# Gated mix of dilated attention and a token-mixing MLP on one core: the gate row spread by GpSimd, the biases loaded by quarters and turned by VectorE

## The chip, the core and the metric

The kernel runs on one core of a Trainium2 chip. A core has a matrix engine (TensorE, PE in the profile, with its weight loads listed as PEld), a vector engine (VectorE, DVE), an engine for functions of one input (ScalarE, ACT), a general engine (GpSimd, POOL) and an engine that here only issues transfers (SyncE, SP). Each has its own queue of instructions and runs them in order; they wait for each other through semaphores. PE writes only to PSUM, which has eight banks; the other data lie in SBUF, with 128 partitions. The metric is the device time of one execution in microseconds (us).

## What is computed

With x of 2048 tokens by 512 channels, the output is `g * a + (1 - g) * b`:

```python
g = _sigmoid((x * gate_w).sum(-1, keepdims=True))     # one gate for each token
# a: 32 heads of 16 channels; token s looks at s, s-2, ..., s-14
qkv = x @ wqkv                                        # 512 -> 1536
logits = einsum("bhsd,bhswd->bhsw", q, kg) * scale    # 8 places, masked where s - 2w < 0
a = einsum("bhsw,bhswd->bhsd", softmax(logits), vg) @ wo
# b: an MLP over the tokens, for each channel
h = _layernorm(x)
u = _gelu(einsum("bsd,sf->bdf", h, w1) + b1)          # 2048 -> 1792
b = transpose(einsum("bdf,fs->bds", u, w2) + b2)      # 1792 -> 2048
```

All inputs and the output are bf16. Two vectors matter here: `gate_w`, 512 values that every partition needs as a row, and the biases `b1` (1792) and `b2` (2048), which the kernel needs as columns: 14 columns of 128 for b1 (B1C) and 16 for b2 (B2C), one value for each partition.

## The kernel before

Tokens lie on the partitions in 16 tiles of 128 (X). PE's program has these stages, in this order: an opening (five warming products, the transposes tx0 to tx3 of the first four x tiles, and the "lead" products, which multiply the first four normalised tiles with the first 512 columns of w1 into banks 0 to 3); the projections of q, k and v (L713); the first MLP product, ph2 (L609), with two short sums over q·k products (sum0 and sum1, L803) in between; and the second MLP product, ph3 (L937), to which the attention output times wo (L946) is added in the same bank. ACT evicts the projections and takes the functions; VectorE multiplies q with shifted k (128 x 4096 elements at a time), does the softmax arithmetic and multiplies attention with shifted v; some of the wide sums are done by GpSimd's accumulating transfers (L831, L901).

The opening is a chain over four tiles. For tile t, VectorE takes statistics (st), their aggregate (ag, L627); ACT makes the reciprocal deviation with two functions (rstd: Ln and Exp); VectorE normalises the tile (ln, L634); PE runs lead t. ACT and VectorE also copy the transposed x tiles out of PSUM (ext0 to ext3, L598 on VectorE); the projections need these copies.

The gate row and the biases come in through the opening too. GpSimd fills a 128 x 512 buffer with zeros (GWZ, L478), ACT's queue loads the gate row into its first partition (L533), PE multiplies it with a matrix of ones, so that each partition gets the row (gwbc, L643, into bank 6), and ACT copies it to GWB (evgw, L656). The biases are loaded as 14 and 16 rows of 128 (B1R and B2R, L534 and L535, on ACT's queue), PE transposes both into bank 7 (L602 and L603, between tx1 and tx2), and VectorE copies them out (L674, L675), right after the last normalised tile. Then VectorE runs the gate's sums z0 to z15 (L756), one for each x tile: a product of the tile with GWB, summed along the row. z0 to z3 come first; z4 and z5, and the statistics st4 and st5, need x tiles 4 and 5, which are loaded later. A small reduction (RP, L679) and the q·k products follow.

The order on each queue is not the order of the code. A planner (`_Sched`) collects all operations with an assumed duration, their reads and writes, a priority and at times a delay, plays them through a model, and gives each engine its list: whichever ready operation can start first, and among those the one with the longest remaining path. Operations named in `after` fix an order only; `reads`, `writes` and `deps` become waits. PE's list is held in the order of the code, apart from the two sums. So a changed duration or dependency on one engine can change the places of operations that the diff does not show: here those of the q·k products among the statistics, and of sum0 and sum1 among the ph2 products.

GpSimd's queue holds, in order: the fills, the affine select that makes the identity (L475), the fills for padding and mask, and then transfers only: the accumulate of the first q·k products (qd0, L831, 2 MB), two more of 1 MB, the spreading of the attention weights (L880) and the accumulates over v (L901). SP's queue holds all other loads.

Of the kernel before, what the change touches and what calls it, by code (L numbers as in the profile page):

```python
# [5 lines left out]
BF16 = mybir.dt.bfloat16  # L6
# [3 lines left out]
AF = mybir.ActivationFunctionType  # L10
# [3 lines left out]
D = 512  # L14
# [4 lines left out]
NST = S // 128  # L19
# [271 lines left out]
class _Mem:  # L291
# [17 lines left out]
    def view(self, name, dtype, dims, extra=0, p0=0, np_=128):  # L309
        base = self.arena[:].bitcast(dtype)  # L310
        pst = base.ap[0][0]
        esz = mybir.dt.size(dtype)
        o = self.off[name]
        assert o % esz == 0
        return bass.AP(base.tensor, p0 * pst + o // esz + extra, [[pst, np_]] + [list(d) for d in dims])


def bass_gated_mix__sliding_local_dilated__mixer_token_mlp__prompt_kernel(nc, A_x, A_wqkv, A_wo, B_x, B_w1, B_b1, B_w2, B_b2, gate_w, out, dbg=None):
    with contextlib.ExitStack() as es:
# [37 lines left out]
        def psub(ap_, p0, np_, offs, dims):  # L357
            pst = ap_.ap[0][0]
            return bass.AP(ap_.tensor, ap_.offset + p0 * pst + offs, [[pst, np_]] + [list(d) for d in dims])
# [51 lines left out]
        E32 = view("E32", FP32, [(1, D)])  # L411
        GWB = view("GWB", BF16, [(1, D)])
        LX = view("LX", BF16, [(D, NLEAD), (1, D)])
        GWZ = view("LOG", BF16, [(1, D)], extra=NLEAD * 128 * GL)
        GW1 = psub(GWZ, 0, 1, 0, [(1, D)])
        JUNK = view("S4", BF16, [(D, 4), (1, D)])
        ZN = view("Z", FP32, [(1, 32)])
        TZ = view("Z", FP32, [(1, 32)], extra=32)
# [4 lines left out]
        ONES4 = view("ONES", BF16, [(0, 4), (1, 128)])  # L423
        RP = view("RP", BF16, [(1, 32)])
        MASK = view("MASK", BF16, [(PAD, NW), (1, PAD)], np_=32)
        B1R = view("ROWS", BF16, [(1, 128)], np_=NFT)
        B2R = view("ROWS", BF16, [(1, 128)], extra=128, np_=NST)
        so = [0]

        def small(n, dims=None, extra=0):  # L430
# [30 lines left out]
        def psb(bank):  # L461
            return ps[:, bank, :].bitcast(BF16)

        def sub(ap_, offs, dims):
            return bass.AP(ap_.tensor, ap_.offset + offs, [list(ap_.ap[0])] + [list(d) for d in dims])
# [4 lines left out]
        def act(o_, i_, f_, **kw):  # L470
            return lambda e: e.activation(out=o_, in_=i_, func=f_, **kw)  # L471
# [3 lines left out]
        A("pool", lambda e: e.affine_select(out=IDENT, in_=ONES, pattern=[[1, 128]], compare_op=ALU.is_equal,  # L475
                                            fill=0.0, base=0, channel_multiplier=-1),
          0.4, reads=["ones"], writes=["ident"], name="ident")
        A("pool", lambda e: e.memset(GWZ, 0.0), 0.4, writes=["gwr"], name="gwz", prio=-50)  # L478
        A("pool", lambda e: e.memset(sub(KH[0], 0, [(KR, 4), (1, PAD)]), 0.0), 0.2, writes=["kpad"], name="kpad")  # L479
        A("pool", lambda e: e.memset(sub(V5, 0, [(VR, 4), (1, PAD)]), 0.0), 0.2, writes=["vpad"], name="vpad")  # L480

# [12 lines left out]
        def load(name, dst, src, nbytes, writes, transpose=False, queue="sp", issue=0.5, order=True, deps=(), reads=()):  # L494
            ds = sch.dsem(name)

            def fn(e):
                if transpose:
                    return e.dma_start_transpose(dst, src)
                return e.dma_start(dst, src)  # L500
            op = sch.dma(queue, fn, nbytes, ds, issue=issue, reads=reads, writes=writes, deps=deps,
                         after=([last_ld[0]] if order and last_ld[0] is not None else []), name=name)
            if order:
                last_ld[0] = op
            return op
# [25 lines left out]
        ld_w("wk01", 1, 0, 2, "wk")  # L531
        ld_w("wk23", 1, 2, 4, "wk2")
        load("gw", GW1, bass.AP(gate_w.tensor, gate_w.offset, [[D, 1], [1, D]]), 1024, ["gwr"], issue=0.4, queue="act", order=False)  # L533
        load("b1", B1R, B_b1.rearrange("(t p) -> t p", p=128), 4096, ["b1r"], issue=0.4, queue="act", order=False)  # L534
        load("b2", B2R, B_b2.rearrange("(t p) -> t p", p=128), 4096, ["b2r"], issue=0.4, queue="act", order=False)  # L535
        ld_w("wq01", 0, 0, 2, "wq")
        ld_x(4, 2)
        ld_w("wq23", 0, 2, 4, "wq2")
# [25 lines left out]
        def f_warm(n, bank):  # L564
# [4 lines left out]
                return ins  # L569
            return fn  # L570

        chain = [None]

        def PE(fn, dur, reads, writes, name, prio=0):
            op = A("pe", fn, dur, reads=reads, writes=writes, after=([chain[0]] if chain[0] is not None else []), name=name, prio=prio)
            chain[0] = op
            return op
# [12 lines left out]
        def tx(t):  # L590
            PE(f_tx(t), 0.4, ["x%d" % t, "ident"], ["b%d" % TXB[t][0]], "tx%d" % t)

        def ext(t, eng, after):
            bank, o = TXB[t]
            src = sub(psb(bank), o, [(128, 4), (1, 128)])
            dst = sub(XT, t * 128, [(S, 4), (1, 128)])
            if eng == "dve":
                return A("dve", lambda e: e.tensor_copy(out=dst, in_=src), 0.42, reads=["b%d" % bank], writes=["xt0_%d" % t], after=after, name="ext%d" % t, prio=-30)  # L598
            return A("act", act(dst, src, AF.Copy), 0.6, reads=["b%d" % bank], writes=["xt0_%d" % t], after=after, name="ext%d" % t, prio=-30)

        def f_tb(e):
            e.transpose(out=psb(7)[:, 512:512 + NFT], in_=B1R, identity=IDENT[0:NFT, 0:NFT])  # L602
            return e.transpose(out=psb(7)[:, 544:544 + NST], in_=B2R, identity=IDENT[0:NST, 0:NST])  # L603

        def f_ph2(ft, bank, s0, s1):
            def fn(e):
# [22 lines left out]
        def rstd(t, after=()):  # L629
            A("act", act(col(SD, t), AG[:, t, 1:2], AF.Ln, bias=1e-5), 0.25, reads=["ag%d" % t], writes=["sd%d" % t], after=after, name="lnl%d" % t, prio=-40)  # L630
            return A("act", act(col(RSTD, t), col(SD, t), AF.Exp, scale=-0.5), 0.25, reads=["sd%d" % t], writes=["rstd%d" % t], name="rs%d" % t, prio=-40)

        def apply(t, after):
            return A("dve", (lambda t_: lambda e: e.tensor_scalar(out=LX[:, t_, :], in0=X[:, t_, :], scalar1=AG[:, t_, 0:1], scalar2=col(RSTD, t_),  # L634
                                                                  op0=ALU.subtract, op1=ALU.mult))(t), 0.41, reads=["rstd%d" % t, "st%d" % t, "x%d" % t],
                     writes=["lx%d" % t], after=after, name="ln%d" % t, prio=-40)

        PE(f_warm(5, 0), 2.1, [], ["b0"], "warm0")
        tx(0)
        tx(1)  # L640
        PE(f_tb, 0.2, ["b1r", "b2r", "ident"], ["b7"], "t_b12")
        tx(2)
        PE(lambda e: e.matmul(ps[:, 6, :], lhsT=WONE, rhs=GWZ, start=True, stop=True), 0.4, ["gwr"], ["b6"], "gwbc")  # L643
        def lead(t):
            PE(f_lead(t), 0.87, ["lx%d" % t, "lw%d" % t], ["b%d" % ft for ft in range(GL)], "lead%d" % t)

# [6 lines left out]
        lead(0)  # L653
        ag = aggr(1, [l0])
        r1 = rstd(1)
        ew = A("act", act(GWB, ps[:, 6, :], AF.Copy), 0.6, reads=["b6"], writes=["gwb"], after=[r1], name="evgw", prio=-50)  # L656
        tx(3)
        s2 = stat(2, [ag])
        l1 = apply(1, [s2])
        lead(1)  # L660
        ag = aggr(2, [l1])
        r2 = rstd(2)
        s3 = stat(3, [ag])
        l2 = apply(2, [s3])
        ag = aggr(3, [l2])
        e1 = ext(1, "act", [r2, e0])
        r3 = rstd(3, [e1])
        ext(2, "act", [r3])
        e3 = ext(3, "dve", [ag])
        l3 = apply(3, [e3])  # L670
        e3 = l3
        lead(2)
        lead(3)
        A("dve", lambda e: e.tensor_copy(out=B1C, in_=psb(7)[:, 512:512 + NFT]), 0.15, reads=["b7"], writes=["b1c"], after=[e3], name="b1c", prio=-20)  # L674
        A("dve", lambda e: e.tensor_copy(out=B2C, in_=psb(7)[:, 544:544 + NST]), 0.15, reads=["b7"], writes=["b2c"], after=[e3], name="b2c", prio=-20)  # L675

        def f_rp(e):
            with nc.allow_low_precision(reason="exact 0/1 indicator sums"):
# [400 lines left out]
```

## Time and profile before

| what | us |
|---|---|
| median of three runs (lowest, highest) | 163.34 (163.06, 163.67) |
| the profiled execution | 162.99 |
| its span, first to last instruction | 161.7 |
| PE busy | 158.7, 98% |
| VectorE busy | 150.9, 93% |
| ACT busy | 77.5, 48% |
| GpSimd busy | 27.2, 17% |

The span is what the profile's times refer to; the 1.3 us between it and the profiled execution lie outside the instructions shown. TensorE ran at its full clock throughout (granted 1.000). A line of the profile gives the source line, the engine, the operation with its shapes, and a count; a line in order of time begins with start and duration. An idle time in brackets stands ahead of the instruction that ended it, with what it waited for. Instructions that only wait, issue a semaphore or load code for an engine are not shown as busy. A transfer's time is given from its issue to its landing.

### The profile page before, as it was taken

What the parts mean: (1) busy time and instruction counts of PE and PEld (TensorE: products, weight loads), DVE (VectorE), ACT (ScalarE), POOL (GpSimd) and SP (SyncE); (2) the same over time, 40 slices, a digit from 0 to 9 for tenths busy, and PEclk for the clock granted to TensorE, in tenths of its full rate; (3) what the DMA queues carried; (4) which work ended last, traced back from release to release, by engine and by line L of the source; (5) the groups of instructions that cost most, each with busy time, mean ns of one, the idle gap of its engine ahead of it and who ended that gap; (6) DMA issues with size and microseconds to landing.
All of it is one profiled execution on the core that took longest, in us unless ns stands there. A gap on an engine that the chain in (4) does not pass through costs nothing.

```text
span 161.7 us, 2009 instructions
## 1 busy us (share of the span) xinstructions
PE 158.7 (98%) x778; PEld 75.9 (47%) x778; DVE 150.9 (93%) x143; ACT 77.5 (48%) x103; POOL 27.2 (17%) x63
## 2 busy tenths in 40 slices
PE   7999999999999999999999999999999999999994
PEld 3455555555554444444444444444444444444652
DVE  2969999999999999999999999999999999999943
ACT  3827666679999381999311344420111111111153
POOL 4000011000000001200792030008580003020000
DMA  4899999999924999999399999999999913949504
GB/s 133 260 228 267 190 295 292 252 212 216 321 92 111 308 292 245 163 296 190 78 321 360 336 298 294 214 311 290 344 206 214 199 50 78 186 109 211 134 32 162
DMA packets 45303, 35.54 MB, mean 220 GB/s; under 512 B 8045, under 2 KB 42094, under 8 KB 45294
## 3 DMA queue, kind: packets, MB, share of 16 engines
q1 hardware_dynamic: 41392, 22.75, 53.4%
q0 software_dynamic: 3696, 12.59, 36.3%
q8 instruction: 6, 0.10, 0.2%
q10 hardware_dynamic: 206, 0.08, 0.2%
q14 instruction: 3, 0.02, 0.0%
HBM read 19.15 MB, written 2.11 MB: 131 GB/s over the span
## 4 chain that ended last, share of the span: by engine, by line
PE 98%; DVE 0%; issue 0%
PE ps L937 30%; PE ps L609 28%; PE ps L713 26%; PE ps L946 9%; PE ps L618 2%; PE ps L568 1%; PE ps L803 1%; PE ps L586 1%; DVE arena L955 0%; PE ps L643 0%; PE ps L602 0%; PE ps L603 0%
## 5 line engine op out<-in xcount | busy, mean ns | idle before, releaser
L468 DVE TENSOR_TENSOR arena<-arena 128x4096 bf16<-128x4096 bf16 (+6 forms) x71 | 125.7, 1807 | 1.5 <-DMA arena<-arena 0.3
L937 PE MATMUL ps<-arena 128*128 128x512 bf16 (+2 forms) x238 | 50.2, 366 | 0.0
L471 ACT ACTIVATE arena<-ps,arena 128x512 bf16<-128x512 f32 (+1 forms) x29 | 20.9, 727 | 55.5 <-PE ps L946 40.6
L609 PE MATMUL ps<-arena 128*128 128x512 bf16 x208 | 45.4, 379 | 0.0
L713 PE MATMUL ps<-arena 128*128 128x512 bf16 x192 | 41.6, 379 | 0.0
L471 ACT ACTIVATE arena<-ps 128x512 bf16<-128x512 f32 (+3 forms) x38 | 31.5, 843 | 14.4 <-PE ps L713 11.2
L937 PEld LDWEIGHTS ps<-arena 128*128 128x128 bf16 x238 | 23.3, 98 | 25.4
L609 PEld LDWEIGHTS ps<-arena 128*128 128x128 bf16 x208 | 20.2, 98 | 24.9 <-issue 0.8
L713 PEld LDWEIGHTS ps<-arena 128*128 128x128 bf16 x192 | 21.7, 113 | 19.7
L880 POOL DMA_DIRECT2D arena<-arena x32 | 17.1, 664 | 23.1 <-DVE arena L468 14.0
L471 ACT ACTIVATE arena<-arena 128x512 bf16<-128x512 bf16 (+6 forms) x27 | 15.2, 565 | 10.1 <-DVE arena L468 9.2
L946 PE MATMUL ps<-arena 128*128 128x512 bf16 (+2 forms) x68 | 15.6, 366 | 0.0
L831 POOL DMA_DIRECT2D arena<-arena x3 | 3.8, 1270 | 62.3 <-DVE arena L468 62.3
L1028 ACT ACT_TABLE_LOAD x9 | 11.5, 1283 | 2.3 <-POOL arena L479 2.2
L756 DVE CUSTOM_DVE_ANT_0 arena<-arena 128x512 bf16<-128x512 bf16 x16 | 10.2, 688 | 1.3 <-DMA arena<-in_A_x_dram 1.3
L901 POOL DMA_DIRECT2D arena<-arena x4 | 4.9, 1226 | 31.4 <-DVE arena L468 31.4
L946 PEld LDWEIGHTS ps<-arena 128*128 128x128 bf16 x68 | 6.6, 98 | 7.2
L775 DVE BATCH_NORM_STATS2 arena<-arena 128x6 f32<-128x512 bf16 x12 | 7.3, 677 | 0.0
L623 DVE BATCH_NORM_STATS2 arena<-arena 128x6 f32<-128x512 bf16 x4 | 2.7, 669 | 2.9 <-DMA arena<-in_A_x_dram 2.9
L955 DVE TENSOR_SCALAR arena<-ps,arena 128x512 bf16<-128x512 f32 (+1 forms) x2 | 1.3, 660 | 3.1 <-PE ps L946 3.0
L618 PE MATMUL ps<-arena 128*128 128x512 bf16 x16 | 4.0, 381 | 0.0
L568 PE MATMUL ps<-const-bfloat16-1.0 128*128 128x512 bf16 x5 | 2.3, 624 | 0.8 <-PEq L1064 0.8
(39 smaller groups left out, 19.0 us busy)
## 6 DMA issues: line engine op xcount, KB each, us to landing
arena<-in_B_w_dram SPq DMA_DIRECT2D x8, 896.0 KB, 13.3
arena<-arena POOLq DMA_DIRECT2D x6, 1024.0 KB, 9.2
arena<-in_B_w_dram SPq DMA_DIRECT2D x5, 1024.0 KB, 8.8
arena<-arena POOLq DMA_DIRECT2D x32, 128.0 KB, 7.3
arena<-arena POOLq DMA_DIRECT2D x1, 2048.0 KB, 17.9
out_dram<-arena SPq DMA_DIRECT2D x15, 128.0 KB, 2.6
arena<-in_B_w_dram SPq DMA_DIRECT2D x2, 768.0 KB, 13.6
arena<-in_A_wqkv_dram SPq DMA_DIRECT2D x4, 256.0 KB, 5.2
```

The lines of the kernel that those rows point to most:

```text
L468: return lambda e: e.tensor_tensor(out=o_, in0=a_, in1=b_, op=op_)
L471: return lambda e: e.activation(out=o_, in_=i_, func=f_, **kw)
L609: ins = e.matmul(ps[:, bank, :], lhsT=W1S[W1AT[ft // 2]][:, st, 128 * (ft % 2):128 * (ft % 2) + 128], rhs=(LX if st < NLEAD else X)[:, st, :],
L618: ins = e.matmul(ps[:, ft, :], lhsT=LW[:, t, 128 * ft:128 * ft + 128], rhs=LX[:, t, :], start=(t == 0), stop=False)
L713: ins = e.matmul(ps[:, bank, :], lhsT=sub(WQKV, dt * 3 * D + tn * D + dl, [(4, 128)]), rhs=XT[:, dt, sb * 512:(sb + 1) * 512], start=(dt = ...
L756: A("dve", (lambda t_: lambda e: e.tensor_tensor_reduce(out=JUNK[:, t_ % 4, :], in0=X[:, t_, :], in1=GWB, scale=1.0, scalar=0.0, op0=ALU.m ...
L775: A("dve", (lambda t_: lambda e: e.bn_stats(out=ST6[:, t_, :], in_=X[:, t_, :]))(t), 0.6, reads=["x%d" % t], writes=["st%d" % t], after=[e ...
L880: prev = sch.dma("pool", (lambda d_, s_: lambda e: e.dma_start(d_, s_))(dst, src), 131072, ds, issue=1.0, reads=["att%d" % h], writes=["av ...
L901: sch.dma("pool", (lambda d_, s_: lambda e: e.dma_start(d_, s_, accum_op=ALU.add, max_dma_last_dim=4096))(sub(PB[b], 0, [(2048, 2), (1, 20 ...
L937: ins = e.matmul(ps[:, bank, 0:c1 - c0], lhsT=W2S[i // 2][:, ft, 128 * (i % 2):128 * (i % 2) + 128], rhs=UT[:, ft, c0:c1], start=(ft == 0) ...
L946: ins = e.matmul(ps[:, bank, 0:c1 - c0], lhsT=OT[:, i // 2, dl, 128 * (i % 2):128 * (i % 2) + 128], rhs=WO[:, dl, c0:c1], start=False, sto ...
L1028: e.preload_act_table_set(want)
```

## The change

The gate row no longer goes through PE. It is still loaded into one partition by ACT's queue; there is no zero fill. GpSimd's `partition_broadcast` writes it to all partitions of GWB. That operation is given a dependency on the last normalised tile of the opening (l3).

The biases leave ACT's queue. After the broadcast GpSimd fills a 128 x 64 buffer (BROW) with zeros and issues eight loads on its own queue: for each quarter of 32 partitions, 14 rows of 32 values of b1 and 16 rows of 32 values of b2. VectorE transposes the buffer in blocks of 32 x 32 (BCOL), so that quarter q of the partitions gets the values 32q to 32q + 31 of each row of 128, and copies the columns to B1C and B2C. The transpose has a delay of 2.0 in the planner.

PE's opening loses the two bias transposes and the product with ones, and gets two filler products of 128 and 256 columns, whose results are not used. ext1 moves ahead of rstd 2 on ACT, and ext3 moves from VectorE to ACT.

In the order that the planner then gives, GpSimd's broadcast, fill and eight loads stand ahead of qd0, and an instruction that loads the code for the broadcast stands before it. VectorE runs RP ahead of z0; after z4 and z5 it runs two q·k products (before: four), the statistics st6 to st9, the bias transpose and the copy of B1C, more statistics, z6 and z7, and only then the other two q·k products of the first pair, which qd0 waits for. PE's sum0 and sum1 stand eight ph2 products later.

```diff
-        GWZ = view("LOG", BF16, [(1, D)], extra=NLEAD * 128 * GL)
-        GW1 = psub(GWZ, 0, 1, 0, [(1, D)])
+        GW1 = view("LOG", BF16, [(1, D)], extra=NLEAD * 128 * GL, np_=1)
...
-        B1R = view("ROWS", BF16, [(1, 128)], np_=NFT)
-        B2R = view("ROWS", BF16, [(1, 128)], extra=128, np_=NST)
+        BROW = view("ROWS", BF16, [(1, 64)])
+        BCOL = view("ROWS", BF16, [(1, 64)], extra=64)
...
-        A("pool", lambda e: e.memset(GWZ, 0.0), 0.4, writes=["gwr"], name="gwz", prio=-50)
...
-        load("b1", B1R, B_b1.rearrange("(t p) -> t p", p=128), 4096, ["b1r"], issue=0.4, queue="act", order=False)
-        load("b2", B2R, B_b2.rearrange("(t p) -> t p", p=128), 4096, ["b2r"], issue=0.4, queue="act", order=False)
...
+        def f_fill(n, bank):
+            return lambda e: e.matmul(ps[:, bank, 0:n], lhsT=WONE, rhs=WROW[:, 0:n], start=True, stop=True)
...
-        def f_tb(e):
-            e.transpose(out=psb(7)[:, 512:512 + NFT], in_=B1R, identity=IDENT[0:NFT, 0:NFT])
-            return e.transpose(out=psb(7)[:, 544:544 + NST], in_=B2R, identity=IDENT[0:NST, 0:NST])
...
         tx(0)
+        PE(f_fill(128, 0), 0.1, [], ["b0"], "fill0")
         tx(1)
-        PE(f_tb, 0.2, ["b1r", "b2r", "ident"], ["b7"], "t_b12")
+        PE(f_fill(256, 0), 0.2, [], ["b0"], "fill1")
         tx(2)
-        PE(lambda e: e.matmul(ps[:, 6, :], lhsT=WONE, rhs=GWZ, start=True, stop=True), 0.4, ["gwr"], ["b6"], "gwbc")
...
-        ew = A("act", act(GWB, ps[:, 6, :], AF.Copy), 0.6, reads=["b6"], writes=["gwb"], after=[r1], name="evgw", prio=-50)
...
-        r2 = rstd(2)
+        e1 = ext(1, "act", [r1, e0])
+        r2 = rstd(2, [e1])
...
-        e1 = ext(1, "act", [r2, e0])
-        r3 = rstd(3, [e1])
-        ext(2, "act", [r3])
-        e3 = ext(3, "dve", [ag])
-        l3 = apply(3, [e3])
+        e2 = ext(2, "act", [r2])
+        r3 = rstd(3, [e2])
+        ext(3, "act", [r3])
+        l3 = apply(3, [ag])
+        gwp = A("pool", lambda e: e.partition_broadcast(GWB, GW1), 0.5, reads=["gwr"], writes=["gwb"], deps=[l3], name="gwb")
+        A("pool", lambda e: e.memset(BROW, 0.0), 0.15, writes=["brow"], after=[gwp], name="brow0")
+        for q_ in range(4):
+            for n_, b_, c_, k_ in (("b1", B_b1, 0, NFT), ("b2", B_b2, 32, NST)):
+                load("%s_%d" % (n_, q_), psub(BROW, 32 * q_, k_, c_, [(1, 32)]), bass.AP(b_.tensor, b_.offset + 32 * q_, [[128, k_], [1, 32]]),
+                     64 * k_, ["%sr%d" % (n_, q_)], queue="pool", issue=1.0, order=False, deps=[gwp], reads=["brow"])
...
-        A("dve", lambda e: e.tensor_copy(out=B1C, in_=psb(7)[:, 512:512 + NFT]), 0.15, reads=["b7"], writes=["b1c"], after=[e3], name="b1c", prio=-20)
-        A("dve", lambda e: e.tensor_copy(out=B2C, in_=psb(7)[:, 544:544 + NST]), 0.15, reads=["b7"], writes=["b2c"], after=[e3], name="b2c", prio=-20)
+        A("dve", lambda e: e.transpose(out=BCOL, in_=BROW), 0.15, reads=["brow"] + ["b%d%s%d" % (n_, "r", q_) for n_ in (1, 2) for q_ in range(4)], writes=["bcol"], after=[e3], name="btr", prio=-30, delay=2.0)
+        A("dve", lambda e: e.tensor_copy(out=B1C, in_=sub(BCOL, 0, [(1, NFT)])), 0.07, reads=["bcol"], writes=["b1c"], name="b1c", prio=-30)
+        A("dve", lambda e: e.tensor_copy(out=B2C, in_=sub(BCOL, 32, [(1, NST)])), 0.07, reads=["bcol"], writes=["b2c"], name="b2c", prio=-30)
```

## The prediction

> **What bounds the kernel now.** I read the page's engine shares first, then the chain that ended last in order of time, then VectorE's instructions in order of time, GpSimd's likewise, and last the DMA issues of the opening.
>
> ```profile
> PE 158.7 (98%) x778; PEld 75.9 (47%) x778; DVE 150.9 (93%) x143; ACT 77.5 (48%) x103; POOL 27.2 (17%) x63
> ```
>
> TensorE (PE) is busy for 98% of the span, VectorE (DVE) for 93%. Chain in order of time (start, us, what):
>
> ```profile
> 4.16 0.12 PE ps L602
> 4.28 0.03 PE ps L603
> 4.30 0.46 PE ps L586 x4
> 4.77 0.22 PE ps L643
> 4.98 0.87 PE ps L618 x4
> ...
> 8.88 41.44 PE ps L713 x192
> ...
> 154.39 5.20 PE ps L946 x28
> ```
>
> From 8.88 on PE runs without a gap, so only two things can move the end: the opening before 8.88, or an input that reaches PE late. VectorE and GpSimd in order of time (start, us, engine, line, what; in brackets the idle time ahead of it):
>
> ```profile
> 1.26 0.20 POOL L474 MEMSET arena<- 128x128 bf16 x1
> 1.54 0.29 POOL L475 TENSOR_SCALAR_AFFINE_SELECT arena<-arena 128x128 bf16<-128x128 bf16 x1
> 2.46 0.14 POOL L480 MEMSET arena<- 128x56 bf16 x1
> 4.34 0.41 DVE L634 TENSOR_SCALAR arena<-arena 128x512 bf16<-128x512 bf16 x1
> 7.37 0.41 DVE L634 TENSOR_SCALAR arena<-arena 128x512 bf16<-128x512 bf16 x1 [0.20 <-ACT arena L471]
> 7.86 0.68 DVE L756 CUSTOM_DVE_ANT_0 arena<-arena 128x512 bf16<-128x512 bf16 x1
> 11.66 0.69 DVE L756 CUSTOM_DVE_ANT_0 arena<-arena 128x512 bf16<-128x512 bf16 x1 [1.27 <-DMA arena<-in_A_x_dram]
> 14.07 0.28 DVE L679 TENSOR_REDUCE arena<-arena 128x32 bf16<-128x128 bf16 x1
> 14.29 8.90 DVE L468 TENSOR_TENSOR arena<-arena 128x4096 bf16<-128x4096 bf16 x4
> 23.51 1.42 POOL L831 DMA_DIRECT2D arena<-arena  x1 [20.91 <-DVE arena L468]
> 153.76 1.94 DVE L468 TENSOR_TENSOR arena<-arena 128x2048 bf16<-128x2048 bf16 x2
> ```
>
> VectorE is the second bound. It waits 1.27 us for x tile 4 at 11.66, starts the q·k products at 14.29, and from there to 155.70 waits only 0.29 us. Its last sum (avc6) ends at 153.76 + 1.94 = 155.70. PE needs it for wo12, the fourth of the final tiles: 154.39 + 3 x 0.867 = 156.99. Less a hand-over of 0.06 us (the normalised tile ends at 7.78, PE's load of it starts at 7.84), **VectorE may be 1.23 us late**; beyond that the end moves one for one.
>
> **The change, part by part.** The sum is made against the profiled execution, 162.99 us (span 161.7 and 1.3 around it); the median of the runs is 163.34, 0.35 above.
>
> *PE's opening.* It loses L602, L603 and L643, 0.12 + 0.03 + 0.22 = 0.37 us, and gains two fillers of 128 and 256 columns, at the 0.216 us pace of 512 columns 0.16. But the first lead product starts when the first normalised tile ends (4.34 + 0.41 = 4.75; it starts at 4.81), and the others wait for later tiles. So nothing is gained; the bound is a gain of 0.21.
>
> *ACT and the evictions.* The gate eviction (evgw) goes and ext3 comes from VectorE, 0.58 us each; ext1 takes the free slot at 5.22, and the last ext still ends at 7.82. The last normalised tile waits for ACT's rstd (7.34), not for the ext3 that stood ahead of it. Zero; the cover is lead3, on PE until 8.88. The b1 and b2 loads leave the first microsecond, where they are 30 of the small packets beside the x tiles; bounds 0 and a gain of 0.05. GpSimd's zero fill goes too (0.46 earlier for all that follows it, so its last fill ends at 2.60 - 0.46 = 2.14); x tile 0, at 2.93, still sets the start.
>
> *The gate row.* Now z0 to z3 on VectorE wait for GpSimd's broadcast, and behind them stand st4, st5, z4, z5 and the q·k products. In the built program's order an instruction without operands stands directly ahead of the broadcast, a reload of GpSimd's code with index 1. Before has the same kind ahead of the affine select, with index 0; there 1.26 + 0.20 = 1.46 to 1.54 leaves it 0.08 us, but that asks for code which may have been in place. Lower bound 0.08. Upper bound: two fetches one after the other, each like the 5.5 us that the 256 KB x load issued in the same stretch took, 11.0. I take 8.4: the longest transfer issued there, the DMA transpose with 7.1 us, plus an engine's change of tables, the 1.28 us of ACT_TABLE_LOAD; this is an estimate, nearer to the upper end since the index differs. It starts at 2.14, ahead of the wait for the last normalised tile (7.78). The broadcast itself I price like the zero fill of the same width, 0.53 (bounds 0.29, the select, and 1.2). So gwb is ready at 2.14 + 8.4 + 0.53 = 11.07, and z0 starts at 11.13, not at 7.86.
> z0 can be late for free: 1.27 us, the wait for x tile 4, and 0.22, because L679 now runs ahead of z0, so up to 7.86 + 1.27 + 0.22 = 9.35. **Late by 11.13 - 9.35 = 1.78 us** at the q·k products (range 0 to 4.4).
> The Trainium skill, GPSIMD Engine Reference, "Instruction dispatch", puts the first call to freshly loaded code at approximately 6 us more. By that the row would be ready at about 8.7 and nothing would be late; no trace here shows such a load yet.
>
> *The biases.* Eight GpSimd DMA issues follow the broadcast. Rows: 0.54 us each (L880 median), 1.06 at most; landing 2.6 to 4.5 us (shortest L880, the small z_scratch stores). The last lands 0.2 + 4.3 + 2.6 = 7.1 to 0.2 + 8.5 + 4.5 = 13.2 us after the broadcast. VectorE's transpose comes two products and four statistics after the q·k start, 5.0 + 4.45 + 2.4 = 11.9 us after the broadcast. Taken as zero (nearest row 0.54); bound 1.3 us.
> The transpose (0.21 by L762) and two copies (0.17 each, 0.08 apart in L674 and L675) move from before the x4 wait into the gapless stretch: 0.29 to 0.55, taken **0.45 us**.
>
> *The order behind it.* The planner now runs only two q·k products first, then statistics. st8 comes at 19.95 and x tile 8 lands at 15.10 + 5.4 = 20.5: up to 0.55 us if nothing was late before, covered by the 1.78 here. The GpSimd accumulate (L831) is issued some 8 us later. It took 17.9 us to land; between its issue and the add that needs it stand z8 to z15 (4.9), small work (0.5), three normalisations (0.9), four products (8.9) and one wide add (4.5), 19.8 us. Zero, with 1.6 to spare. PE's two sums move behind eight more matmuls, 1.73 us. VectorE's inputs to them were 56.3 - 55.44 = 0.86 and 91.1 - 89.68 = 1.4 us early, so they now bear 2.6 and 3.1.
>
> *Sum.* 1.78 + 0.45 - 1.23 = 1.00. 162.99 + 1.00 = 163.99; with the 0.35 of the median, **164.3 us**.
>
> **Rivals.**
> - *The reload is hidden* (not slower). With up to 6.6 us of reload z0 starts by 9.35. VectorE is then late by 0.55 + 0.45 = 1.0, inside its 1.23: 163.3. It decides at 7.4 us of reload, where 2.23 falls to 1.23; up to 8.2 it stays within 0.8 us. For it speaks the 0.08 us gap; against it, the DMA engines are 71% busy up to 9 us. The skill's 6 us, above, falls here.
> - *Both reloads cost.* If the second index is still in place when the next execution starts, the first reload no longer takes 0.08 us. With 8.4 us for each the identity is ready at 9.7 and PE reaches L713 at 15.1, 6.2 late; z0 starts at 19.45, VectorE is 10.1 + 0.45 late, and the end moves 9.3: 172.7. With 5.5 each it is 166.9. Before, with one index, can't show it.
> - *The accumulate is late.* At twice the longest 1 MB landing (2 x 10.9 us, and 0.3 to issue) it misses the add by 2.3 us; with the reload hidden: 1.0 + 2.3 - 1.23 = 2.1, 165.4. Against it, the SP loads that shared its window are further on by then.
> - *Faster*: at most 0.21 + 0.05 from the opening, 163.1.
>
> **How the numbers follow.** About 0.5%, 0.8 us, is what a measurement of this kernel can tell from no change. Forecast 0.38 (its own range 164.1 to 166.9, the upper bound of the reload: 4.38 + 0.45 - 1.23 = 3.6), hidden 0.38, both reloads 0.16, accumulate or biases late 0.05, faster by more than 0.5% 0.03 (beyond the bound above; only if one of my covers is wrong). So slower 0.59, same 0.38, faster 0.03. The range runs from 162.9 to 168.0 and leaves out the upper part of both reloads and the faster case, under 0.2.
>
> **What the new profile would show.** L756 first at about 11.1 us, with GpSimd as its releaser; a gap on GpSimd from 2.1 to 10.5; q·k from about 16.1; wo12 waiting for VectorE about 1 us near 157. If L756 starts near 8.5 the reload is hidden. If the affine select starts later than 2 us, both reloads cost, and the forecast is wrong by far. If VectorE idles ahead of its StreamTranspose or of a 128x8192 add, the biases or the accumulate are late.

## The result and the profile after

The changed kernel takes 169.81 us (median of four runs, 169.57 to 169.93), the kernel before on the same chip 163.2 (162.98 to 163.67). The ratio is 1.0401, with a 95% interval of 1.0385 to 1.0417: it is **slower by 4%**, outside the predicted range of 162.9 to 168.0. The profiled execution took 169.57 us, with a span of 168.3, 6.58 us more than the 162.99 of the profiled execution before.

The engine shares of the profile after:

```profile
span 168.3 us, 2000 instructions
PE 158.5 (94%) x762; PEld 76.6 (45%) x777; DVE 150.8 (90%) x143; ACT 77.7 (46%) x103; POOL 31.8 (19%) x72
```

PE has as much to do as before (158.5 against 158.7 us) and its share falls from 98% to 94%, so the new time is idling. Where it idles is told by the chain that ended last, in order of time (start, us, what):

```profile
0.80 0.20 POOL arena L473
...
1.07 7.70 issue
8.77 0.29 POOL arena L474
...
9.11 0.61 PE ps L585 x4
...
10.89 1.71 PE ps L613 x4
12.60 0.27 PE ps L585 x4
12.87 2.59 PE ps L613 x12
15.46 2.16 PE ps L714 x10
...
162.32 3.86 PE ps L947 x21
166.20 0.51 DVE arena L956
```

L474 is the affine select that makes the identity, L585 the transposes of the opening, L613 the lead products, L714 the first projections (L713 before). The projections start at 15.46 instead of 8.88, **6.58 us later**, and the last VectorE instruction of the chain starts at 166.20 instead of 159.62, again 6.58 later. So the whole loss arises before the projections; behind them nothing is lost or won. Ahead of the affine select stand 7.70 us of "issue", time in which GpSimd waits for nothing that the profile names. GpSimd in order of time, with idle time in brackets:

```profile
0.80 0.20 POOL L473 MEMSET arena<- 128x128 bf16 x1 [0.29 <-POOLq L1065]
8.77 0.28 POOL L474 TENSOR_SCALAR_AFFINE_SELECT arena<-arena 128x128 bf16<-128x128 bf16 x1 [7.76 <-issue]
...
9.70 0.13 POOL L478 MEMSET arena<- 128x56 bf16 x1
15.66 0.55 POOL L665 PARTITION_BROADCAST arena<-arena  x1 [5.83 <-issue]
16.06 0.26 POOL L666 MEMSET arena<- 128x64 bf16 x1
16.64 4.43 POOL L498 DMA_DIRECT2D arena<-in_B_b_dram  x8 [0.31 <-POOL arena L666]
38.78 1.40 POOL L832 DMA_DIRECT2D arena<-arena  x1 [17.71 <-DVE arena L467]
```

There are two such waits, at the two places where the built program has an instruction that loads GpSimd code: 7.76 us ahead of the affine select (index 0) and 5.83 ahead of the broadcast (index 1). Before, the first of the two took at most 0.08 us. VectorE in order of time shows what each wait leaves behind:

```profile
10.71 0.41 DVE L629 TENSOR_SCALAR arena<-arena 128x512 bf16<-128x512 bf16 x1 [5.21 <-ACT arena L470]
...
12.89 0.41 DVE L629 TENSOR_SCALAR arena<-arena 128x512 bf16<-128x512 bf16 x1 [0.50 <-ACT arena L470]
13.22 0.28 DVE L680 TENSOR_REDUCE arena<-arena 128x32 bf16<-128x128 bf16 x1
16.25 0.69 DVE L757 CUSTOM_DVE_ANT_0 arena<-arena 128x512 bf16<-128x512 bf16 x1 [2.75 <-POOL arena L665]
...
151.97 10.60 DVE L467 TENSOR_TENSOR arena<-arena 128x8192 bf16<-128x8192 bf16 x6
```

The second normalised tile starts at 10.71 after 5.21 us of waiting, since ScalarE's copy of the first transposed tile, which needs the identity, stands ahead of the next reciprocal root in its queue. z0 (L757) starts at 16.25, not at 7.86. VectorE's last sum ends at 151.97 + 10.60 = 162.57, against 155.70: 6.87 late. PE itself is 6.58 late and VectorE had 1.23 to spare, so up to 7.81 would have cost nothing: the second load hides behind the first with 0.94 us left, and PE's opening sets the time.

### The profile page after: what moved, and what is told of

Read it like the earlier page. It is cut to its first block, busy times and chain, and to the rows that moved or that the text cites. A ratio compares the mean times of both kernels' runs of the same rounds, so it can differ in the third digit from the quotient of the medians.

```text
span 168.3 us, 2000 instructions
## 1 busy us (share of the span) xinstructions
PE 158.5 (94%) x762; PEld 76.6 (45%) x777; DVE 150.8 (90%) x143; ACT 77.7 (46%) x103; POOL 31.8 (19%) x72
## 4 chain that ended last, share of the span: by engine, by line
PE 88%; issue 5%; ACT 5%; DVE 0%; POOL 0%; POOLq 0%
PE ps L938 29%; PE ps L604 27%; PE ps L714 19%; PE ps L947 8%; ACT arena L470 5%; PE ps L613 3%; PE ps L804 1%; PE ps L585 1%; DVE arena L956 0%; PE ps L569 0%; POOL arena L474 0%; POOL arena L473 0%; POOLq L474 0%; POOLq L1065 0%
## 5 line engine op out<-in xcount | busy, mean ns | idle before, releaser
L604 PE MATMUL ps<-arena 128*128 128x512 bf16 x203 | 45.0, 379 | 0.4 <-issue 0.2
L714 PE MATMUL ps<-arena 128*128 128x512 bf16 x188 | 41.4, 379 | 0.2
L938 PEld LDWEIGHTS ps<-arena 128*128 128x128 bf16 x238 | 23.3, 98 | 25.4
L604 PEld LDWEIGHTS ps<-arena 128*128 128x128 bf16 x208 | 20.2, 98 | 24.9 <-issue 0.4
L714 PEld LDWEIGHTS ps<-arena 128*128 128x128 bf16 x192 | 21.7, 113 | 19.7
L757 DVE CUSTOM_DVE_ANT_0 arena<-arena 128x512 bf16<-128x512 bf16 x16 | 10.2, 688 | 2.8 <-POOL arena L665 2.8
L947 PEld LDWEIGHTS ps<-arena 128*128 128x128 bf16 x68 | 6.6, 98 | 7.2
L585 PE MATMUL ps<-arena 128*128 128x128 bf16 x16 | 2.3, 297 | 6.0 <-POOL arena L474 6.0
L629 DVE TENSOR_SCALAR arena<-arena 128x512 bf16<-128x512 bf16 x4 | 1.6, 412 | 5.8 <-ACT arena L470 5.7
L585 PEld LDWEIGHTS ps<-arena 128*128 128x128 bf16 x16 | 1.8, 142 | 7.5 <-POOL arena L474 6.9
## 6 DMA issues: line engine op xcount, KB each, us to landing
arena<-arena POOLq DMA_DIRECT2D x1, 2048.0 KB, 14.2
```

The lines of the kernel that those rows point to most:

```text
L585: ins = e.transpose(out=psb(bank)[:, o + dt * 128:o + dt * 128 + 128], in_=X[:, t, dt * 128:(dt + 1) * 128], identity=IDENT)
L604: ins = e.matmul(ps[:, bank, :], lhsT=W1S[W1AT[ft // 2]][:, st, 128 * (ft % 2):128 * (ft % 2) + 128], rhs=(LX if st < NLEAD else X)[:, st, :],
L714: ins = e.matmul(ps[:, bank, :], lhsT=sub(WQKV, dt * 3 * D + tn * D + dl, [(4, 128)]), rhs=XT[:, dt, sb * 512:(sb + 1) * 512], start=(dt = ...
L757: A("dve", (lambda t_: lambda e: e.tensor_tensor_reduce(out=JUNK[:, t_ % 4, :], in0=X[:, t_, :], in1=GWB, scale=1.0, scalar=0.0, op0=ALU.m ...
L938: ins = e.matmul(ps[:, bank, 0:c1 - c0], lhsT=W2S[i // 2][:, ft, 128 * (i % 2):128 * (i % 2) + 128], rhs=UT[:, ft, c0:c1], start=(ft == 0) ...
L947: ins = e.matmul(ps[:, bank, 0:c1 - c0], lhsT=OT[:, i // 2, dl, 128 * (i % 2):128 * (i % 2) + 128], rhs=WO[:, dl, c0:c1], start=False, sto ...
```

## The experiments

Three theories were open. **A**: GpSimd keeps the code that an execution leaves in place; the changed program ends with index 1, the next execution starts by asking for index 0, and so both loads are paid each time, while a program with one index finds it in place. **B**: in a program that asks for two indices each load costs its full price, whatever stands there at the start. **C**: the wait ahead of the affine select is no code load; something else that the change moved holds GpSimd.

**restore0: the changed kernel, which loads index 0 again at its end.**

```diff
+        nc.gpsimd.load_library(library_config.all_libraries[0])
+        nc.gpsimd.memset(TAIL, 0.0)
```

The two lines stand behind GpSimd's last transfer; TAIL is a small buffer of its own.

> The changed kernel; behind GpSimd's last transfer the code with index 0 is loaded again, then a small fill shows when that load is done. Theory A (the code that an execution leaves is what the next one finds, so both reloads cost): the affine select is back at about 1.1 us, only the second reload is left, from about 2.0 to between 7.8 and 9.8; z0 at 8.4 to 10.4; VectorE is at most 1.0 + 0.5 late at the q.k products; the time is 163.0 to 163.7. Theory B (a program with two indices pays for each reload, whatever is in place at its start): the select stays near 8.8 and the time at 169.5 to 170. Theory C (the first wait is no reload): as B.

Measured: 163.62 us (163.29 to 164.36, ten runs) against 163.3 for the kernel before on the same chip, ratio 1.0011 (0.9991 to 1.0030). GpSimd in order of time:

```profile
1.30 0.29 POOL L477 TENSOR_SCALAR_AFFINE_SELECT arena<-arena 128x128 bf16<-128x128 bf16 x1 [0.29 <-POOL arena L476]
...
8.63 0.55 POOL L668 PARTITION_BROADCAST arena<-arena  x1 [6.26 <-DVE arena L683]
...
152.80 0.12 POOL L1054 MEMSET arena<- 128x32 bf16 x1 [7.24 <-issue]
```

The affine select is back at 1.30, and the 7 us are now at the end (7.24 ahead of the last fill), where nobody waits for GpSimd. With nothing else altered, the 6 us of loss are gone. This is against B and C. The second load is still there, and the broadcast starts at 8.63. The idle time is put down to VectorE's L683, but that begins at 7.91 and without a load the broadcast comes 0.18 us behind that instruction's start (7.95 against 7.77 in onelib, below), so here the load ended last.

**before_leave1: the kernel before, which loads index 1 at its end.**

```diff
+        nc.gpsimd.load_library(library_config.all_libraries[1])
+        nc.gpsimd.memset(TAIL, 0.0)
```

> The kernel before, untouched, but behind GpSimd's last transfer the code with index 1 is loaded, which nothing uses. Theory A: the next execution pays for index 0 in its opening: affine select near 9.2 (1.46 + 7.8), projections from about 15.4, time 169 to 170.5, although no work was added in front of any other. Theory B: with two indices in the program the same. Theory C: nothing changes, 163.2.

Measured: 171.23 us (170.72 and 171.74), ratio 1.0467 (1.0413 to 1.0522). GpSimd in order of time:

```profile
9.46 0.28 POOL L478 TENSOR_SCALAR_AFFINE_SELECT arena<-arena 128x128 bf16<-128x128 bf16 x1 [7.99 <-issue]
...
158.16 0.12 POOL L1053 MEMSET arena<- 128x32 bf16 x1 [6.09 <-issue]
```

Its chain that ended last, at the first transposes and the first projections:

```profile
9.80 1.04 PE ps L589 x8
...
16.60 1.94 PE ps L716 x9
```

Nothing of the change is in this kernel: only what it leaves in place for the next execution is another index. The wait of 7.99 us ahead of the affine select appears, and with it the loss: the projections start at 16.60 against 8.88, 7.72 us later, and the profiled execution (170.72) is 7.73 us longer. Together with restore0 this shows A: the price is paid at the start, for what the execution before left. The loss is larger than I expected (169 to 170.5 us, projections from about 15.4): the select starts at 9.46 instead of 9.2, and from the first transpose to the projections it takes 6.80 us, against 5.84 in the kernel before; in part of them PE ran slowly (four lead products take 1.91 us instead of 1.03), which later runs look into.

**onelib: the changed kernel with index 1 throughout.** Index 1 has the affine select too, so it serves for both.

```diff
+        nc.gpsimd.load_library(library_config.all_libraries[1])
         emit_engine("pool", nc.gpsimd)
```

> The changed kernel with the code of index 1 asked for at the start, which holds both the select and the broadcast, so index 0 is never loaded. Theory A: index 1 is always in place, no reload costs anything: select at about 1.1, broadcast right behind the last normalised tile (about 7.9), z0 at about 8.5, time 162.9 to 163.4. If each execution started with index 0 instead, one reload of 5.8 to 7.8 us would stand ahead of the select: 168.5 to 170.

Measured: 163.45 us (162.97 to 164.76, ten runs), ratio 1.0008 (0.9981 to 1.0036). GpSimd:

```profile
1.24 0.29 POOL L475 TENSOR_SCALAR_AFFINE_SELECT arena<-arena 128x128 bf16<-128x128 bf16 x1
...
7.95 0.55 POOL L666 PARTITION_BROADCAST arena<-arena  x1 [5.65 <-DVE arena L630]
```

No load is paid at either place; the broadcast waits for the last normalised tile alone, and z0 starts at 8.53. The waits of VectorE for x tiles come into view again (0.71 us at 11.78, 0.79 at 25.07), the second at a place where I had not looked for one. The time is level with before, 0.05 us above the range that I expected: rid of both loads, the change gives back nothing either.

**biasonly: the changed kernel with the gate row spread by PE as before.**

```diff
-        gwp = A("pool", lambda e: e.partition_broadcast(GWB, GW1), 0.5, reads=["gwr"], writes=["gwb"], deps=[l3], name="gwb")
+        gwp = l3
...
+        PE(lambda e: e.matmul(ps[:, 6, :], lhsT=WONE, rhs=GWZ, start=True, stop=True), 0.4, ["gwr"], ["b6"], "gwbc")
...
+        ew = A("act", act(GWB, ps[:, 6, :], AF.Copy), 0.6, reads=["b6"], writes=["gwb"], after=[r1], name="evgw", prio=-50)
```

> The changed kernel with the gate row as before (zero fill, product with ones, eviction by ACT) and the new bias path. No code with index 1. Theory A: 163.0 to 163.5; VectorE is 0.3 to 1.0 us late, inside its 1.23. If the bias path has a cost of its own (eight GpSimd issues, the transpose's wait), VectorE idles ahead of its StreamTranspose and the time is above 163.7.

Measured: 163.76 us (163.3 to 164.69, ten runs), ratio 1.0021 (1.0000 to 1.0041). VectorE in order of time around the bias transpose:

```profile
19.04 1.87 DVE L780 BATCH_NORM_STATS2 arena<-arena 128x6 f32<-128x512 bf16 x3
20.83 0.23 DVE L678 STREAM_TRANSPOSE arena<-arena 128x64 bf16<-128x64 bf16 x1
21.09 0.17 DVE L679 CAST arena<-arena 128x14 f32<-128x14 bf16 x1
```

There is no wait ahead of the transpose: the eight late loads have landed. But the median is above the 163.0 to 163.5 that I expected, and 0.06 above the 163.7 that was to be one half of the sign of a cost. The profiled execution, 0.33 us longer than that of the kernel before, shows this time elsewhere. Its third normalised tile waits for ScalarE, which here copies the gate row and the second transposed tile ahead of the root:

```profile
6.70 0.41 DVE L631 TENSOR_SCALAR arena<-arena 128x512 bf16<-128x512 bf16 x1 [0.22 <-ACT arena L471]
```

The projections start at 9.22, 0.34 later than before. So no cost of the new path of the biases is shown; the ratio leaves room for 0.4% at most.

**gateonly: the changed kernel with the biases as before**, so that only the gate row goes the new way. The transposed biases go to bank 6, which is free without the gate product. The 128-column filler and the new order of the copies stay.

```diff
+        load("b1", B1R, B_b1.rearrange("(t p) -> t p", p=128), 4096, ["b1r"], issue=0.4, queue="act", order=False)
+        load("b2", B2R, B_b2.rearrange("(t p) -> t p", p=128), 4096, ["b2r"], issue=0.4, queue="act", order=False)
...
-        PE(f_fill(256, 0), 0.2, [], ["b0"], "fill1")
+        PE(f_tb, 0.2, ["b1r", "b2r", "ident"], ["b6"], "t_b12")
...
-        A("pool", lambda e: e.memset(BROW, 0.0), 0.15, writes=["brow"], after=[gwp], name="brow0")
```

> Before with the gate row spread by GpSimd alone: the biases are loaded and transposed by TensorE as before, with the matmul and the copy for the gate row gone. The program asks for both code indices, as the changed one does. By theory A (the index that the last execution left in place has to be loaded over) the time is that of the changed kernel: affine select at 8.5 to 9.6, time 169.5 to 170.4 (the two bias transposes stand in the slow stretch, up to 0.3 more). If the eight bias loads on GpSimd's queue or VectorE's transpose had a share in the loss, it is below 169.3.

Measured: 170.42 us (169.87 to 170.53, four runs), ratio 1.0417 (1.0382 to 1.0452).

```profile
8.52 0.28 POOL L474 TENSOR_SCALAR_AFFINE_SELECT arena<-arena 128x128 bf16<-128x128 bf16 x1 [7.52 <-issue]
...
15.48 0.55 POOL L671 PARTITION_BROADCAST arena<-arena  x1 [5.90 <-issue]
```

The new way of the gate row carries the loss without that of the biases, as A has it. The median is 0.02 above my bound, for a reason that the next two runs show.

These left a remainder. In the changed kernel the affine select ends 7.22 us later than before (9.05 against 1.83) and the first transpose starts 6.07 us later (9.11 against 3.04), but the projections 6.58. From the first transpose to the projections the changed kernel takes 6.35 us, the kernel before 5.84. The next two runs tell apart theory X, the order of copies and roots on ScalarE, and theory P, slow matmuls on PE.

**extlate: the changed kernel with the four copies behind the last reciprocal root on ScalarE.**

```diff
-        e0 = ext(0, "act", [r0])
...
-        e1 = ext(1, "act", [r1, e0])
-        r2 = rstd(2, [e1])
+        r2 = rstd(2)
...
-        e2 = ext(2, "act", [r2])
-        r3 = rstd(3, [e2])
-        ext(3, "act", [r3])
+        r3 = rstd(3)
+        e0 = ext(0, "act", [r3])
+        e1 = ext(1, "act", [e0])
+        e2 = ext(2, "act", [e1])
+        ext(3, "act", [e2])
```

> In the changed kernel the opening from the first transpose (9.11) to the projections (15.46) took 6.35 us, against 5.84 (3.04 to 8.88) before. Two theories for that half microsecond. Theory X (ScalarE's order): the four copies of the transposed tiles stand between the reciprocal roots on ScalarE's queue, the first copy cannot start before 9.75, and so the normalised tiles 1 to 3 come late (10.71 to 13.30). Here the four copies stand behind the last root: normalised tiles 1 to 3 are done before 9.1, and if X is right the projections start 0.5 to 1.0 us earlier, near 14.6 to 15.0, and the time is 168.9 to 169.3. Theory P (TensorE's pace): TensorE is busy without a gap from 9.11, and it is its matmuls that are slow: the four 512-column products at 10.68 took 1.91 us, 0.43 us each from start to start, against 1.03 before, after six microseconds of idling, though the granted clock is shown as 1.00. By P nothing moves: projections at 15.3 to 15.5, time 169.7 to 169.9.

Measured: 170.59 us (169.65 to 170.6, four runs), ratio 1.0424 (1.0388 to 1.0461). PE in order of time (start, us, line, shape, count):

```profile
8.98 0.61 PE L585 MATMUL ps<-arena 128*128 128x128 bf16 x4 [5.85 <-POOL arena L474]
...
10.56 1.91 PE L613 MATMUL ps<-arena 128*128 128x512 bf16 x4
12.26 0.63 PE L585 MATMUL ps<-arena 128*128 128x128 bf16 x4
12.69 3.80 PE L613 MATMUL ps<-arena 128*128 128x512 bf16 x12
16.33 1.89 PE L714 MATMUL ps<-arena 128*128 128x512 bf16 x8
```

The last normalised tile now starts at 7.39, and yet PE is no earlier: X falls for this kernel. P held in its kind, not in its number: I had said that nothing moves, and the projections came 1.0 us later (16.33 against 15.29 in the same view of the changed kernel), because the slow pace of PE went on longer. Products of 512 columns started 0.43 us apart until about 14.8, 5.8 us behind the first transpose; in the changed kernel the pace had doubled by 12.6, 3.5 us behind it. In gateonly it lasted until about 14.7, 5.9 us behind its first transpose: that is its excess (projections at 16.41 in its chain, against 15.46). One of the four runs of extlate took 169.65 and three 170.58 to 170.60, so the length of the slow stretch probably also differs between executions of one kernel; only one execution has a trace.

**warmlong: the changed kernel with 31 opening matmuls without use in place of 5**, so that PE does not idle during the load.

```diff
-        PE(f_warm(5, 0), 2.1, [], ["b0"], "warm0")
+        PE(f_warm(31, 0), 2.1, [], ["b0"], "warm0")
```

> The changed kernel with 31 opening matmuls of 512 columns without use in place of 5, so that TensorE is busy until about 8.7 to 9.1 while GpSimd's first code load goes on. By P (slow matmuls because TensorE had idled) the products at 10.7 then take about 1.0 us for four in place of 1.91, the transposes their warm pace, and the projections start 0.9 to 1.3 us earlier, at 14.2 to 14.6: time 168.5 to 169.0. By X (ScalarE's order of copies and roots) the opening still takes 6.3 us from the first transpose and the time stays at 169.7 to 170.0. In both, the first code load of 7 to 8 us stays, so the time stays far above that before.

Measured: 169.43 us (169.11 to 169.48, four runs), ratio 1.0364 (1.0337 to 1.0390). PE in order of time:

```profile
0.84 9.48 PE L564 MATMUL ps<-const-bfloat16-1.0 128*128 128x512 bf16 x31 [0.84 <-PEq L1065]
10.16 0.38 PE L585 MATMUL ps<-arena 128*128 128x128 bf16 x4
...
10.99 1.03 PE L613 MATMUL ps<-arena 128*128 128x512 bf16 x4
...
12.08 2.98 PE L613 MATMUL ps<-arena 128*128 128x512 bf16 x12
14.89 3.40 PE L714 MATMUL ps<-arena 128*128 128x512 bf16 x15
```

Same operations, same data: four lead products take 1.03 us, as before the change, and not 1.91. From the first transpose to the projections it is 14.89 - 10.16 = 4.73 us; by the same view the changed kernel took 15.29 - 9.11 = 6.18. That is P. The time fell by only 0.4 us, short of what I expected, for two reasons that the trace shows. I had counted the matmuls at the fast pace, but the early ones ran at the slow one, so they held back the transposes until 10.16, 1.5 us after the affine select had ended (8.39 + 0.28). And with PE earlier, VectorE sets the end: z0 starts at 16.59, and the chain that ended last now runs through VectorE's sums:

```profile
160.69 1.84 DVE arena L467 x2
...
162.55 0.70 DVE arena L467
...
163.30 2.79 PE ps L947 x16
```

So once the first load is bridged in part, the second, behind which z0 waits, comes to bear.

**onelib_order: onelib, with the copies of tiles 1 to 3 behind the last reciprocal root**, the one version that might have been faster than both kernels.

```diff
+        nc.gpsimd.load_library(library_config.all_libraries[1])
...
-        e1 = ext(1, "act", [r1, e0])
-        r2 = rstd(2, [e1])
+        r2 = rstd(2)
...
-        e2 = ext(2, "act", [r2])
-        r3 = rstd(3, [e2])
-        ext(3, "act", [r3])
+        r3 = rstd(3)
+        e1 = ext(1, "act", [r3, e0])
+        e2 = ext(2, "act", [e1])
+        ext(3, "act", [e2])
```

> The changed kernel with one code index throughout (index 1 loaded at the start) and the copies of tiles 1 to 3 behind the last reciprocal root on ScalarE. With one index the last normalised tile waited 0.51 us for ScalarE (7.44). Here it should start near 7.0, the last lead products end up to 0.2 us earlier, and the projections start at 8.7 to 9.1, not before 8.7. Expected level with before, 163.0 to 163.6: without the code loads the change gives nothing back. If it is faster than before by more than 0.5% (below 162.5), the change had a gain that the loads had hidden.

Measured: 163.48 us (163.07 to 163.78, ten runs) against 163.39, ratio 1.0002 (0.9986 to 1.0018). The time is level as expected, but not for my reason. VectorE's last normalised tile:

```profile
7.38 0.41 DVE L630 TENSOR_SCALAR arena<-arena 128x512 bf16<-128x512 bf16 x1 [0.51 <-ACT arena L471]
```

It still waits 0.51 us for ScalarE with no copy in between, so that wait is the way through the root itself. And PE:

```profile
4.82 1.64 PE L614 MATMUL ps<-arena 128*128 128x512 bf16 x4
...
9.37 8.80 PE L715 MATMUL ps<-arena 128*128 128x512 bf16 x40
```

The first four lead products took 1.64 us instead of 1.03 (before: 1.03 at 4.82), part of them at the slow pace, and the projections start at 9.37, outside my 8.7 to 9.1. The slow pace is only about half of that: the last twelve lead products start 0.23 us later than in onelib (6.52 against 6.29), the projections 0.50 (9.37 against 8.87). The rest is a wait: the weights of the first projection are loaded at 9.34, after 0.57 us of idling that the profile puts down to ScalarE, whose last copy, moved back by this edit, ended at 8.80. No version ran faster than the kernel before.

## Why the prediction was wrong

- **The failed step** stands in the part on the gate row: of the first load it says "1.26 + 0.20 = 1.46 to 1.54 leaves it 0.08 us, but that asks for code which may have been in place", and then the sum keeps 0.08 for it (its last fill ends at 2.14). What the sentence names was so: the code had been in place, left by the execution before. But the changed program leaves the other index, so that row's condition is gone in exactly this kernel. The step should have been priced like the second load. It was worth 7.76 us ahead of the affine select, of which 6.58 us reached the end, and set the whole result; before_leave1 and restore0 show it from both sides.
- The rival "both reloads cost" came true, by its own mechanism, and its own sign appeared: the affine select at 8.77, later than 2 us. Its price of 8.4 us for each load was above the 7.76 and 5.83 measured, its time of 172.7 too high, and the measured 169.81 lies within its 166.9 to 172.7. It reckoned VectorE to be the one that ends last; with the shorter second load it is PE, for which it had 5.4 us from the identity to the projections (9.7 to 15.1), measured 6.41 (9.05 to 15.46). The fault was its chance of 0.16. Nothing in the profile of before could show that a second index keeps the first from being in place, but the argument for the 0.08 us already contained it.
- **Size of the load.** Taken 8.4 us, measured 5.83 for the load that the sum prices. The case "hidden" was worked out for up to 6.6 us with z0 by 9.35, VectorE late by 1.0, and 163.3. With the first load away (restore0) that is what came: z0 at 9.22, VectorE's last sum 0.85 late (it ends at 145.95 + 10.60 = 156.55, before at 155.70), 163.62 against 163.3 for the kernel before. Had the first load cost nothing, this rival would have been right and the forecast 0.7 too high. The Trainium skill, GPSIMD Engine Reference, "Instruction dispatch", says approximately 6 us more for the first call to freshly loaded code; the trace agrees for the index of the broadcast (5.83), and shows more for the other (7.76).
- **Broadcast**: taken 0.53, measured 0.55.
- **Biases**: eight issues in 4.43 us, 0.55 each (taken 0.54); no wait ahead of VectorE's transpose in the changed kernel or in biasonly. Zero held; gateonly, without the new path, gains nothing back.
- **Accumulate**: zero held (the times listed for its 19.8 us add up to 19.7, which changes nothing). Its transfer landed 14.2 us after its issue (before 17.9), and VectorE waits ahead of no wide add.
- **PE's opening and ScalarE**, taken at nothing. Where no load holds back the identity, the projections of the profiled executions start at 9.04 (onelib), 9.17 (restore0), 9.22 (biasonly) and 9.37 (onelib_order) against 8.88. So no gain was overlooked, and there is a loss of 0.16 to 0.49 us that the sum did not have; the medians stay level all the same. Behind a load it was 0.51 us net, with PE at its slow pace, a term that the prediction, and the rival too, did not have.
- **VectorE's slack** of 1.23 us fits: 6.87 late against PE's own 6.58, and the end moved by 6.58. In warmlong it was used up: VectorE's last sum ends 7.55 late (163.25), PE's projections start 6.17 late (14.89 against 8.72 in the same view), and the profiled execution is 6.49 longer, near 7.55 - 1.23 = 6.32.

## What to carry to other kernels

An operation that needs other code on an engine is to be priced twice: once where it is called, and once at the first call of the next execution, which finds what the last one left; a gap of almost nothing in the profile of before tells only that the code was in place. When the choice is free, take all operations of that engine from one set of code, or put the return to the first set where the engine has nothing to do (here 7.24 us of it cost nothing). A delay of TensorE's first work can grow on its way, because the matmuls behind it run slowly for some microseconds: here 6.07 us at the first transpose became 6.58 at the projections.

## What the runs showed of the hardware

- **Code stays in place on GpSimd between executions.** With the index already there the affine select follows after 0.08 us in the kernel before and 0.29 in restore0, which the profile puts down to the fill ahead of it. A change of index took 5.83 to 7.99 us, shown as idle time without a releaser.
- **The price went with the index, not with the stretch.** The six loads of index 0 (over index 1) took 7.24 to 7.99 us: 7.24 near the end of restore0, 7.39 to 7.99 in an opening. The loads of index 1 (over index 0) with nothing else to wait for took 5.83, 5.90, 5.91 and 6.54 in the opening and 6.09 near the end of before_leave1. In restore0 a load of index 1 began at 2.37, in the opening stretch in which the others load index 0, and took at most 6.26. I had argued from busy DMA engines for a long load; the two groups do not overlap, while the places do. Why they differ was not tried.
- **PE's pace after idling.** After 5.97 us without work, products of 512 columns started 0.43 us apart instead of 0.216, for 3.5 us in the changed kernel, 4.0 in before_leave1 and 5.8 or 5.9 in extlate and gateonly; what sets the length was not tried. The kernel before starts like that too: its five warming products take 2.29 us, 0.46 each, although its clock is given as 1.000, so that figure does not stand for the full pace throughout:

```profile
0.84 2.29 PE L568 MATMUL ps<-const-bfloat16-1.0 128*128 128x512 bf16 x5 [0.84 <-PEq L1064]
```

The granted clock shows nothing of it in the changed kernel either:

```profile
PEclk9999999999999999999999999999999999999999
```

In this row a 9 stands for 90% or more. One slice is 4.2 us, and the slow stretch fills most of the third; the row sees nothing of it, the duration of one matmul does. In extlate, whose slow stretch reaches into the fourth slice, the mean granted clock is 1.000 as well. The Trainium skill, TensorE: Matmul & The Clock Gate, "Part 1: The HAM clock gate (the "warmup" mystery)", has such a rule: an idle array runs at half its clock until about 3.4 us of sustained work, counted in windows that run freely. The paces agree, 0.43 and 0.216, and so does the 3.5 us of the changed kernel; the 5.8 us of extlate lies beyond the 0.5 us of spread that it names.
